# Two row groups of the last down weights on four DMA engines, in a two-layer decode kernel

## The chip, the cores and the metric

The kernel runs on one core of one Trainium2 chip. The metric is the device time of one execution in microseconds (us), the median of several runs. A core has TensorE (PE; its weight loads are PEld), VectorE (DVE), ScalarE (ACT), GpSimd (POOL) and SyncE (SP), and 16 DMA engines that bring data from HBM to SBUF. SyncE issues the loads here.

## The reference

Two sequences (B = 2) go through one token of two equal layers, each an attention over a cache (A) and a gated MLP (B), all in float32:

```python
x = x + _A_ref(_layernorm(x), A_k_cache, A_v_cache, A_wq, A_wo)   # 32 heads, 8192 keys, 128 wide
x = x + _B_ref(_layernorm(x), B_w_gate, B_w_up, B_w_down)         # 576 -> 4608 -> 576
x = x + _A_ref(_layernorm(x), A_k_cache, A_v_cache, A_wq, A_wo)
x = x + _B_ref(_layernorm(x), B_w_gate, B_w_up, B_w_down)

def _B_ref(x, w_gate, w_up, w_down):
    h = _gelu(x @ w_gate) * (x @ w_up)
    return h @ w_down
```

The same weights and caches serve both layers, and do not fit on the chip, so they are read twice: 1151 MB in all.

## The kernel before, in words

All loads go into one large buffer, `space` (128 partitions). A planner in Python, `Space`, holds a queue of loads with the place that each wants; `pump` issues the first of the queue as soon as the program that has been written so far frees its place, and never one ahead of another. So the order of the loads is the order in which they are put into the queue, and SyncE (which issues them) and the 16 DMA engines take them in that order. A load has one of eight semaphores in turn, so it also waits until the load eight issues before it has landed. The names in the rows of order below, DMAHW0 to DMAHW7, are these.

The change touches the very end, the down projection of the second layer. The hidden vector has 4608 numbers per sequence. They lie as 4 tiles (NT) of 128 partitions by 9 row groups (NI): hidden number t*1152 + 9*p + i is in tile t, partition p, group i. The weights of one row group of a tile are 128 rows of 576 (D) floats, one row a partition. `last_down` cuts the tiles into pieces, one load each: tile 0 whole (9 groups), tile 1 whole, tile 2 in two parts (groups 0 to 4, groups 5 to 8), tile 3 in five (0 to 3, 4 to 5, 6, 7, 8). `down` loads a piece: every partition of the 128 gets its groups one behind the other.

`lower` uses a piece up: for each group four matmuls, one for each 144 (CW) columns of the output, with the activations `hT` (128 partitions by 2 sequences) as weights and the piece as moving data, all added up in the PSUM bank `xps`. A float32 matmul counts as two instructions in the trace, each with a weight load. `hidden` makes `hT` from the sums of gate and up, on VectorE and ScalarE. `hT[1]` holds tiles 2 and 3. Line 996 adds `xps` to x, and two stores end the program.

`idle` lists fillers (line 990): matmuls on nothing of use, that keep TensorE busy behind a piece. Before, two of 256 columns stand behind the first part of tile 2, three behind the second, one of 160 behind the first part of tile 3.

Of the kernel before, what the change touches and what calls it, by code (L numbers as in the profile page):

```python
# [15 lines left out]
P = 128  # L16
B = 2
# [3 lines left out]
D = 576  # L21
# [4 lines left out]
HALF = P // 2  # L26
# [9 lines left out]
NI = 9  # L36
NT = 4
CW = D // 4
# [6 lines left out]

P0, P1, P2 = 0, 8 * PART, 16 * PART
HELD = 4 * DH
END = 25 * PART + 768 - HELD
MID = 19 * PART
MIDEND = END - 3 * PART + HELD  # L50
LATE = END - 4 * PART

# [79 lines left out]
def decode_layers(ctx, tc, x_in, kc, vc, wq, wo, wg, wu, wd, out):  # L132
    nc = tc.nc
# [6 lines left out]

    space = consts.tile([P, END], F32, name="space")
    sp = Space()
    at_of = {}
# [12 lines left out]
    def done(key):  # L156
        sp.free(key)
        sp.pump()
# [16 lines left out]
    def runs(where, a, n):  # L175
        return where.runs(a, n) if isinstance(where, Flow) else [(0, a, n)]

    def rows(key, w, width, where, first, size):

        def load(a):  # L180
            at_of[key] = a
            for off, to, n in runs(where, a, size):
                src = bass.AP(w.tensor, w.offset + first + off, [[18 * width, HALF], [10 * width, 2], [1, n]])
                nc.sync.dma_start(space[:, to:to + n], src)

        sp.queue.append((key, where, size, load))
# [34 lines left out]
    def down(key, where, piece):  # L221
        (t, lo), (last_t, _), n = piece[0], piece[-1], len(piece)

        def load(a):
            at_of[key] = a
            if last_t == t:
                src = wd[t * P * NI:(t + 1) * P * NI, :].rearrange("(p i) c -> p (i c)", i=NI)
                for off, to, m in runs(where, a, n * D):
                    nc.sync.dma_start(space[:, to:to + m], src[:, lo * D + off:lo * D + off + m])
            else:  # L230
                src = bass.AP(wd.tensor, wd.offset + (t * P * NI + lo) * D, [[NI * D, P], [P * NI * D, n], [1, D]])
                nc.sync.dma_start(space[:, a:a + n * D].rearrange("p (t c) -> p t c", t=n), src)

        sp.queue.append((key, where, n * D, load))

    def out_rows(key, where, g, lo=0, hi=GH):

        def load(a):
            at_of[key] = a
            src = wo[g * GH * DH:(g + 1) * GH * DH, :].rearrange("(p i) c -> p (i c)", i=GH)  # L240
            nc.sync.dma_start(space[:, a:a + (hi - lo) * D], src[:, lo * D:hi * D])

        sp.queue.append((key, where, (hi - lo) * D, load))
# [12 lines left out]
    def run(t, lo, hi):  # L256
        return [(t, i) for i in range(lo, hi)]

    first_down = [run(t, lo, lo + 3) for t in range(NT) for lo in range(0, NI, 3)]
    last_down = [run(t, 0, 9) for t in range(NT - 2)] + [run(NT - 2, *r) for r in ((0, 5), (5, 9))]  # L260
    last_down += [run(NT - 1, *r) for r in ((0, 4), (4, 6), (6, 7), (7, 8), (8, 9))]
    downs = first_down, last_down
    idle = {(1, NT - 2, 0): (256, 256), (1, NT - 2, 5): (256, 256, 256), (1, NT - 1, 0): (160,)}


    cache("k", 0, pairs[0], slots0[0], 0, 4)
# [26 lines left out]
    for g in range(NG):  # L293
        for lo in range(0, GH, 2):
            out_rows(("wo", 0, g, lo), mid, g, lo, lo + 2)
# [29 lines left out]
    for n, item in enumerate(pairs[::-1]):  # L325
        for m, kind in enumerate("kv"):
            at = slots1[(2 * n + m) % 3]
# [7 lines left out]
    for n, g in enumerate(range(NG)[::-1]):  # L335
        out_rows(("wo", 1, g, 0), n * GH * D if n < NG - 1 else P2, g)

    big = sp.ring(0, END)

# [4 lines left out]
    for off, n in ((0, 4), (4, 2), (6, 2)):  # L344
        rows(("u", 1, off), wu, HF, big, off * HF, n * HF)
    for piece in downs[1]:
        down(("d", 1) + piece[0], big, piece)


    ident = consts.tile([P, P], F32, name="ident")  # L350
# [60 lines left out]
    scores = consts.tile([P, P], F32, name="scores")  # L411
# [12 lines left out]
    sm = [psum1.tile([P, 512], F32, name="sm%d" % s) for s in range(2)]  # L424
    xps = psum1.tile([P, 512], F32, name="xps")
# [11 lines left out]
    def spin(bank, k=1):  # L437
        for _ in range(k):
            nc.tensor.matmul(bank[0:B, 3 * P:4 * P], of[:, 0:B], ident, start=True, stop=True)
# [52 lines left out]
    def attention(layer, items, apart):  # L492
# [134 lines left out]
        def base_of(kind, item, k):  # L627
            return at_of[key_of(kind, item, k)[:-1]] + k * PART

        def multiply(n, unit):  # L630
# [6 lines left out]
            at = base_of("k", item, lo)  # L637
            r0 = HELD // DH if layer == 1 and n == 0 and lo == 1 else 0
            to = at
# [166 lines left out]
        for n in range(last + 1):  # L806
# [4 lines left out]
            for k, unit in enumerate(units):  # L811
# [8 lines left out]
                if layer == 0 and n == last and k == 1:  # L820
                    sp.trim(("k", 0) + s3.name + (1,), HELD)
                if k == 0:
# [64 lines left out]
    def mlp(layer, apart):  # L887
# [13 lines left out]
        hT = [turns[:, 2 * NI * B * k:2 * NI * B * (k + 1)].rearrange("p (t r) -> p t r", r=B) for k in range(2)]  # L901
# [33 lines left out]
        def lower(piece):  # L935
            key = ("d", layer) + piece[0]
            for k, (t, i) in enumerate(piece):
                for c in range(4):
                    a = at_of[key] + k * D + c * CW
                    a = a if layer else flow.fold(a)  # L940
                    nc.tensor.matmul(
                        xps[32 * c:32 * c + B, 0:CW], hT[t // 2][:, t % 2 * NI + i, :], space[:, a:a + CW],
                        start=piece == downs[layer][0] and k == 0,
                        stop=piece == downs[layer][-1] and k == len(piece) - 1,
                    )
            done(key)

        if layer == 0:
            for half in range(2):
                for g, name in enumerate("gu"):  # L950
                    for i in range(NW):
                        for s in range(2):
                            key = name, 0, half, i, s
# [11 lines left out]
        else:  # L965
# [16 lines left out]
            for half in range(2):  # L982
                hidden(half)
        flat = prz.rearrange("p g e r -> p (g e r)")
        for piece in downs[layer]:
            lower(piece)
            if layer == 0:
                spin(qp[1], 2 if piece == downs[0][-1] else 1)
            for n in idle.get((layer,) + piece[0], ()):
                nc.tensor.matmul(sm[0][0:B, 0:n], hT[1][:, 0, :], flat[:, 0:n], start=True, stop=True)  # L990

    attention(0, forward, turn(True))
    mlp(0, turn())
    attention(1, backward, turn())
    mlp(1, turn())
    nc.vector.tensor_add(x, xps[:, 0:CW], x)
    for b, queue in enumerate((nc.sync, nc.scalar)):
# [28 lines left out]
```

## Time and profile before

| | us |
|---|---|
| median of three runs | 2684.74 |
| lowest and highest | 2684.34, 2685.34 |
| the profiled execution | 2684.92 |
| its span, from the first to the last instruction | 2683.1 |
| mean granted TensorE clock in it | 0.642 |

The profile is of one execution. Engine rows give the busy time, and in brackets what ended the idle time before. Rows of the windows view stand for one stretch of time each: its length, the busy time and count of PE, PEld, DVE, ACT and POOL, TensorE's granted clock as a share of full speed, the mean busy share of the 16 DMA engines, and what they moved in GB/s. The share is a mean: it tells how many engines work, not which. Rows with the name of a queue (q1 are the loads that SyncE issues) give packets, MB, and the share of the time of 16 engines.

### The profile page before, as it was taken

To read this page: it belongs to the slowest core of one execution; us is meant where nothing else is said; L and a number is where in the kernel's file an instruction comes from. 1 tells how busy PE (TensorE), PEld (TensorE's weight loads), DVE (VectorE), ACT (ScalarE), POOL (GpSimd) and SP (SyncE) were. 2 spreads that over 40 slices of the span, in tenths; PEclk is the share of its full clock that TensorE was granted. 3 is DMA by queue.
4 is the path that set the end of the run, shared out by engine and by line. 5 is a ranking of instruction groups with operands and counts; after the bars stand their busy time and mean duration, and the time that the engine had idled before them with its cause. 6 is when DMAs were issued, how large, how long until landed. Compare 5 with 4: busy or idle time off the path is not lost.

```text
span 2683.1 us, 18551 instructions
## 1 busy us (share of the span) xinstructions
PE 933.1 (35%) x7356; PEld 327.5 (12%) x7356; DVE 1864.7 (69%) x1358; ACT 180.8 (7%) x919; POOL 1143.3 (43%) x341
## 2 busy tenths in 40 slices
PE   1332332233233223326664233233323332332256
PEld 0110110011001101102221011001100110110022
DVE  5578777867777787787158777787677778767851
ACT  0000000000000000003013100000000000000000
POOL 2345444544544454454014444454454445435530
PEclk7656665666566566656986666566656656665667
DMA  9999999999999999999999999999999999999998
GB/s 422 435 436 427 433 435 433 434 430 434 432 433 434 431 432 437 433 427 421 406 407 442 430 429 434 436 434 425 436 437 432 430 434 434 432 434 430 433 424 374
DMA packets 37767, 1152.29 MB, mean 429 GB/s; under 512 B 4256, under 2 KB 4912, under 8 KB 16304
## 3 DMA queue, kind: packets, MB, share of 16 engines
q1 hardware_dynamic: 37656, 1151.09, 99.8%
q8 instruction: 58, 0.95, 0.1%
q14 instruction: 29, 0.24, 0.0%
q10 hardware_dynamic: 24, 0.01, 0.0%
HBM read 1151.08 MB, written 0.00 MB: 429 GB/s over the span
## 4 chain that ended last, share of the span: by engine, by line
DMA 26%; DVE 13%; PE 8%; POOL 6%; issue 1%; ACT 1%; POOLq 0%; SPq 0%; ACTq 0%; DVEq 0%
DMA space<-in_A_k_cache_dram 18%; DVE space L645 7%; POOL space L649 6%; PE acc L740 6%; DVE scores L662 4%; DMA space<-in_B_w_down_dram 3%; DMA space<-in_B_w_gate_dram 1%; DMA space<-in_B_w_up_dram 1%; DMA space<-in_A_v_cache_dram 1%; DMA space<-in_A_wo_dram 1%; DMA space<-in_A_wq_dram 1%; DVE osb L758 1%; ACT prz L710 1%; PE sm L720 0%; PE xps L785 0%
## 5 line engine op out<-in xcount | busy, mean ns | idle before, releaser
L649 POOL TENSOR_TENSOR space<-space 128x2048 f32<-128x2048 f32 (+3 forms) x331 | 1139.8, 3452 | 1314.2 <-DVE space L645 1183.8
L645 DVE TENSOR_TENSOR space<-space,qp 128x4096 f32<-128x4096 f32 (+1 forms) x331 | 1133.1, 3439 | 462.1 <-DMA space<-in_A_k_cache_dram 448.3
L662 DVE TENSOR_REDUCE scores<-space 128x32 f32<-128x2048 f32 (+3 forms) x331 | 581.6, 1757 | 115.1 <-POOL space L649 112.2
L740 PE MATMUL acc<-space,prz 128*8 128x512 f32 x4096 | 593.0, 741 | 8.0 <-issue 6.4
L769 PE MATMUL spare<-small,osb 128*64 128x2 f32 (+1 forms) x528 | 70.8, 256 | 1197.3 <-ACT osb L760 1180.1
L769 PEld LDWEIGHTS spare<-small,osb 128*64 128x64 f32 (+1 forms) x528 | 65.2, 208 | 1213.9 <-ACT osb L760 1195.1
L740 PEld LDWEIGHTS acc<-space,prz 128*8 128x8 f32 x4096 | 113.3, 103 | 422.4 <-issue 418.1
L694 PE MATMUL sm<-ident,small 128*1 128x128 f32 x66 | 24.3, 368 | 329.0 <-DVE small L692 329.0
L760 ACT COPY osb<-osb 128x128 f32<-128x128 f32 x60 | 17.9, 298 | 1730.4 <-DVE osb L758 1730.4
L758 DVE SCALAR_TENSOR_TENSOR osb<-acc,small,osb 128x128 f32<-128x128 f32 x204 | 71.6, 351 | 7.2
L476 POOL TENSOR_TENSOR small<-small 128x2 f32<-128x2 f32 x4 | 2.8, 699 | 165.2 <-DVE small L475 165.2
L720 PE MATMUL sm<-small 128*128 128x2 f32 x120 | 34.9, 361 | 81.0 <-ACT prz L710 81.0
L652 ACT ACTIVATE space<-space 128x128 f32<-128x128 f32 x188 | 55.6, 297 | 64.5 <-DVE space L645 51.9
L710 ACT ACTIVATE prz<-scores,small 64x128 f32<-64x128 f32 (+1 forms) x136 | 53.3, 392 | 3.2
L694 PEld LDWEIGHTS sm<-ident,small 128*1 128x1 f32 x66 | 5.2, 79 | 339.2 <-DVE small L692 309.1
L701 PE MATMUL sm<-small 1*128 1x2 f32 (+1 forms) x132 | 38.2, 356 | 22.7 <-DVE small L699 22.7
L720 PEld LDWEIGHTS sm<-small 128*128 128x128 f32 x120 | 29.8, 308 | 86.2 <-ACT prz L710 86.2
L699 DVE TENSOR_REDUCE small<-sm 1x2 f32<-1x128 f32 (+1 forms) x66 | 18.4, 279 | 31.1 <-PE sm L694 31.1
L756 DVE TENSOR_SCALAR osb<-acc,small 128x128 f32<-128x128 f32 x68 | 23.3, 342 | 23.7 <-PE acc L740 23.7
L706 ACT ACTIVATE small<-sm 128x2 f32<-128x2 f32 (+1 forms) x66 | 11.3, 172 | 390.1 <-PE sm L701 390.1
L701 PEld LDWEIGHTS sm<-small 1*128 1x128 f32 x132 | 32.5, 304 | 40.9 <-DVE small L699 40.7
L913 DVE STREAM_TRANSPOSE turned<-acc 128x288 f32<-128x288 f32 x4 | 1.9, 483 | 49.3 <-PE acc L895 49.2
(159 smaller groups left out, 448.1 us busy)
## 6 DMA issues: line engine op xcount, KB each, us to landing
space<-in_A_k_cache_dram SPq DMA_DIRECT2D x8, 4096.0 KB, 15.0
space<-in_A_v_cache_dram SPq DMA_DIRECT2D x3, 4096.0 KB, 20.9
space<-in_A_v_cache_dram SPq DMA_DIRECT2D x6, 2048.0 KB, 20.8
space<-in_B_w_gate_dram SPq DMA_DIRECT2D x18, 576.0 KB, 8.4
space<-in_B_w_up_dram SPq DMA_DIRECT2D x18, 576.0 KB, 7.8
space<-in_A_wo_dram SPq DMA_DIRECT2D x16, 576.0 KB, 8.1
space<-in_A_wo_dram SPq DMA_DIRECT2D x8, 1152.0 KB, 31.2
space<-in_B_w_gate_dram SPq DMA_DIRECT2D x2, 4608.0 KB
```

Of the source, the lines that this page charges most:

```text
L645: nc.vector.tensor_tensor(out=u, in0=t, in1=qp_of(n)[:, 0:DH].unsqueeze(1).to_broadcast([P, j - r0, DH]), op=ALU.mult)
L649: nc.gpsimd.tensor_tensor(out=half, in0=half, in1=u[:, :m - r0, DH // 2:], op=ALU.add)
L652: nc.scalar.activation(row, row, AF.Copy, accum_out=S[n][:, 16 * lo + r:16 * lo + r + 1])
L662: nc.vector.tensor_reduce(out=S[n][:, r0:r1], in_=half, axis=AX.X, op=ALU.add)
L694: nc.tensor.transpose(peaks[n], m, ident)
L701: nc.tensor.matmul(low[n], one[0:1, :].to_broadcast([1, P]), m1, start=True, stop=True)
L710: nc.scalar.activation(prz[rows_, 0:item.rows // 4, e, :], s[rows_, 0:item.rows].rearrange("p (g r) -> p g r", r=4), AF.Exp, bias=nbs[rows ...
L720: nc.tensor.matmul(tot, ones, rs[:, n % 2, :], start=True, stop=True)
L740: nc.tensor.matmul(acc_of(n)[32 * c:32 * c + 8, :], prz[:, g, :, :].rearrange("p e r -> p (e r)"), space[:, at:at + 4 * DH], start=(g < 4) ...
L756: nc.vector.tensor_scalar_mul(t, q[:, 0, :], diag[:, 0:1])
L758: nc.vector.scalar_tensor_tensor(t, q[:, r, :], diag[:, r:r + 1], t, op0=ALU.mult, op1=ALU.add)
L769: nc.tensor.matmul(to[:, i, 0:item.heads], t[:, i:item.heads * DH:GH], w, start=True, stop=True,)
```

## The change

Groups 7 and 8 of tile 2 (FEW = 2) leave the second piece of that tile. `few_rows` brings them to 32 partitions instead of 128: two loads, j = 0 and 1, each to 16 partitions (0 to 15 and 32 to 47), where each partition gets four pieces of 1152 floats, from four rows of the source that follow each other. The source is laid out as 4 x 16 x 1152, so that its outer dimension is 4. They stand in the queue between the two parts of tile 2.

The weights are now in other partitions, so the activations have to go there too. `choose_few` does it, ahead of tile 1: eight small matmuls with every fourth column of the unit matrix as weights pick out the activations of 16 partitions at a time into a PSUM bank, and two copies on VectorE bring them to `few`, a part of the `scores` buffer, which was cleared ahead. `lower_few`, ahead of the second part of tile 2, is then 32 matmuls of 48 partitions (16 to 31 count as zero) instead of 8 of 128. The fillers behind tile 2's parts go, and six of 256 columns stand behind tile 0.

```diff
+FEW = 2
...
+    def few_rows(key, where, t):
+
+        def load(a):
+            at_of[key] = a
+            for j in range(2):
+                first = (t * P + j * HALF) * NI + NI - FEW
+                src = bass.AP(wd.tensor, wd.offset + first * D, [[16 * NI * D, 4], [NI * D, 16], [1, FEW * D]])
+                nc.sync.dma_start(space[32 * j:32 * j + 16, a:a + 4 * FEW * D], src)
+
+        sp.queue.append((key, where, 4 * FEW * D, load))
...
-    last_down = [run(t, 0, 9) for t in range(NT - 2)] + [run(NT - 2, *r) for r in ((0, 5), (5, 9))]
+    last_down = [run(t, 0, 9) for t in range(NT - 2)] + [run(NT - 2, *r) for r in ((0, 5), (5, NI - FEW))]
...
-    idle = {(1, NT - 2, 0): (256, 256), (1, NT - 2, 5): (256, 256, 256), (1, NT - 1, 0): (160,)}
+    idle = {(1, 0, 0): 6 * (256,), (1, NT - 1, 0): (160,)}
...
     for piece in downs[1]:
+        if piece[0] == (NT - 2, 5):
+            few_rows(("few", 1), big, NT - 2)
         down(("d", 1) + piece[0], big, piece)
...
+        few = scores[:, 0:4 * FEW * B].rearrange("p (s i b) -> p s i b", i=FEW, b=B)
+
+        def choose_few():
+            nc.vector.memset(few, 0.0)
+            every = sm[1][:, 0:4 * FEW * B].rearrange("p (s i b) -> p s i b", i=FEW, b=B)
+            for j in range(2):
+                for s in range(4):
+                    nc.tensor.matmul(
+                        every[32 * j:32 * j + 16, s, :, :].rearrange("p i b -> p (i b)"),
+                        ident[:, HALF * j + s:HALF * j + HALF:4],
+                        hT[1][:, NI - FEW:NI, :].rearrange("p i b -> p (i b)"), start=True, stop=True,
+                    )
+                nc.vector.tensor_copy(few[32 * j:32 * j + 16], every[32 * j:32 * j + 16])
+
+        def lower_few():
+            at = at_of["few", 1]
+            for s in range(4):
+                for i in range(FEW):
+                    for c in range(4):
+                        a = at + (s * FEW + i) * D + c * CW
+                        nc.tensor.matmul(
+                            xps[32 * c:32 * c + B, 0:CW], few[0:48, s, i, :], space[0:48, a:a + CW],
+                            start=False, stop=False,
+                        )
+            done(("few", 1))
+
         for piece in downs[layer]:
+            if layer == 1 and piece[0] == (1, 0):
+                choose_few()
+            if layer == 1 and piece[0] == (NT - 2, 5):
+                lower_few()
             lower(piece)
```

How this moves the loads on SyncE, from the first part of tile 2 (128x2880) on; first the rows of before.

```order
L229 DMA space<-in_B_w_down_dram 128x2880 [waits DMAHW6_49,DVE_49,PE_49]
L229 DMA space<-in_B_w_down_dram 128x2304 [waits DMAHW7_49,DVE_49]
L229 DMA space<-in_B_w_down_dram 128x2304 [waits DMAHW0_49]
L229 DMA space<-in_B_w_down_dram 128x1152 [waits DMAHW1_49]
L229 DMA space<-in_B_w_down_dram 128x576 [waits DMAHW2_49,PE_49]
L229 DMA space<-in_B_w_down_dram 128x576 [waits DMAHW3_49,PE_49]
L229 DMA space<-in_B_w_down_dram 128x576 [waits DMAHW4_49,PE_49]
```

And the same place of the changed kernel, again on SyncE.

```order
L230 DMA space<-in_B_w_down_dram 128x2880 [waits DMAHW6_49,DVE_49,PE_49]
L244 DMA space<-in_B_w_down_dram 16x4x1152 [waits DMAHW7_49,DVE_49]
L244 DMA space<-in_B_w_down_dram 16x4x1152 [waits DMAHW0_49]
L230 DMA space<-in_B_w_down_dram 128x1152 [waits DMAHW1_49]
L230 DMA space<-in_B_w_down_dram 128x2304 [waits DMAHW2_49,PE_49]
L230 DMA space<-in_B_w_down_dram 128x1152 [waits DMAHW3_49,PE_49]
L230 DMA space<-in_B_w_down_dram 128x576 [waits DMAHW4_49,PE_49]
L230 DMA space<-in_B_w_down_dram 128x576 [waits DMAHW5_49,PE_49]
L230 DMA space<-in_B_w_down_dram 128x576 [waits DMAHW6_49,PE_49]
```

The two loads of 16 partitions stand ahead of what is left of tile 2, and each load behind them waits for a semaphore that is two places further on: the last two now for DMAHW5 (tile 1) and DMAHW6 (first part of tile 2).

On TensorE, behind tile 0, the rows of before: tile 1 from the wait for DMAHW5 on, tile 2, and its fillers (L990).

```order
L941 MATMUL xps<-space,turns 2x144 [waits DMAHW5_49]
L941 MATMUL xps<-space,turns 2x144 x35
L941 MATMUL xps<-space,turns 2x144 [waits DMAHW6_49,DVE_49]
L941 MATMUL xps<-space,turns 2x144 x15
L941 MATMUL xps<-space,turns 2x144 [waits Pool_49]
L941 MATMUL xps<-space,turns 2x144 x3
L990 MATMUL sm_112<-prz,turns 2x256 x2
L941 MATMUL xps<-space,turns 2x144 [waits DMAHW7_49]
L941 MATMUL xps<-space,turns 2x144 x10
L941 MATMUL xps<-space,turns 2x144 [waits Pool_49]
L941 MATMUL xps<-space,turns 2x144 x4
L990 MATMUL sm_112<-prz,turns 2x256 x3
```

The same place of the changed kernel, from the last rows of fillers behind tile 0 (L1034) to the end of tile 2; L1006 is `choose_few`, L1019 `lower_few`, `scores` holds `few`.

```order
L1034 MATMUL sm_112<-prz,turns 2x256 x5
L1006 MATMUL sm_113<-turns,ident 16x4 x4
L1006 MATMUL sm_113<-turns,ident 16x4 [waits DVE_49]
L1006 MATMUL sm_113<-turns,ident 16x4 x3
L955 MATMUL xps<-space,turns 2x144 [waits DMAHW5_49]
L955 MATMUL xps<-space,turns 2x144 x35
L955 MATMUL xps<-space,turns 2x144 [waits DMAHW6_49]
L955 MATMUL xps<-space,turns 2x144 x15
L1019 MATMUL xps<-space,scores 2x144 [waits DMAHW7_49,DMAHW0_49,DVE_49]
L1019 MATMUL xps<-space,scores 2x144 x10
L1019 MATMUL xps<-space,scores 2x144 x20
L955 MATMUL xps<-space,turns 2x144 [waits DMAHW1_49]
```

Between tile 0 and tile 1 there are now fillers and the eight matmuls of `choose_few`, with a wait for VectorE's first copy in their middle; behind the first part of tile 2 the moved groups take the place of two fillers.

## The prediction

> **What bounds the kernel now.** I read the page first, its DMA parts above all. (The first row names the span. Under 3 stand queue: packets, MB, share of the time of 16 DMA engines.)
>
> ```profile
> span 2683.1 us, 18551 instructions
> ...
> PE 933.1 (35%) x7356; PEld 327.5 (12%) x7356; DVE 1864.7 (69%) x1358; ACT 180.8 (7%) x919; POOL 1143.3 (43%) x341
> ...
> q1 hardware_dynamic: 37656, 1151.09, 99.8%
> q8 instruction: 58, 0.95, 0.1%
> ...
> HBM read 1151.08 MB, written 0.00 MB: 429 GB/s over the span
> ```
>
> The loads (q1) fill 99.8% of 16 engines' span, and no compute engine is over 69%. So the kernel is bound by DMA from end to end, and one DMA engine moves 429/16 = 26.8 GB/s. What is left to look at is the end. The chain that ended last:
>
> ```profile
> 2659.16 20.18 DMA space<-in_B_w_down_dram
> 2679.34 0.04 issue
> 2679.38 0.47 PE xps L941 x8
> 2679.85 0.02 issue
> 2679.87 0.31 DVE x L996
> ```
>
> The last row group of the down weights lands at 2679.34, eight TensorE instructions use it up, and one addition follows. Nothing but the arrival of the last bytes sets the end. Now the same end second by second; the last two columns are the mean share of 16 DMA engines that is busy, and GB/s, and the column before them is TensorE's granted clock.
>
> ```profile
> 2621.00:2671.00 50.00, 29.01 (x382) 12.00 (x374) 6.53 (x31) 0.47 (x2) 0.70 (x1) 0.70 1.00 423
> 2671.00:2672.00 1.00, 1.00 (x32) 0.64 (x26) 0.00 (x0) 0.00 (x0) 0.00 (x0) 0.70 0.98 394
> 2672.00:2673.00 1.00, 1.00 (x30) 0.60 (x19) 0.00 (x0) 0.00 (x0) 0.00 (x0) 1.00 0.82 336
> 2673.00:2674.00 1.00, 1.00 (x29) 0.71 (x31) 0.00 (x0) 0.00 (x0) 0.00 (x0) 1.00 0.66 270
> 2674.00:2675.00 1.00, 1.00 (x17) 0.54 (x13) 0.00 (x0) 0.00 (x0) 0.00 (x0) 1.00 0.59 228
> 2675.00:2676.00 1.00, 1.00 (x13) 0.31 (x14) 0.00 (x0) 0.00 (x0) 0.00 (x0) 1.00 0.58 217
> 2676.00:2677.00 1.00, 1.00 (x34) 0.77 (x26) 0.00 (x0) 0.00 (x0) 0.00 (x0) 1.00 0.55 217
> 2677.00:2678.00 1.00, 0.94 (x23) 0.36 (x24) 0.00 (x0) 0.00 (x0) 0.00 (x0) 1.00 0.18 71
> 2678.00:2679.00 1.00, 0.72 (x16) 0.17 (x16) 0.00 (x0) 0.00 (x0) 0.00 (x0) 1.00 0.11 41
> 2679.00:2680.00 1.00, 0.52 (x12) 0.11 (x8) 0.13 (x1) 0.00 (x0) 0.00 (x0) 1.00 0.06 16
> ```
>
> All 16 engines work until 2671 or so. Then the share falls in steps: 0.59 of 16 is nine engines, 0.11 is two. So **seven engines are done between 2671.5 and 2674.5, seven more near 2677, and two go on to about 2678.8**. All have the same bytes to move; they end 7 us apart. The shares after 2671 add up to 4.53 us: with the bytes dealt out evenly all would end at 2675.5, some 3.3 us before the last does now. **No shifting of bytes among engines can gain more than that**, 0.12% of the span.
>
> **The change, part by part.** The times are those of the profiled execution: 2683.1 us of span in a run of 2684.92, against a median of 2684.74 for three runs. I work out differences and set them off from the median.
>
> *The bytes.* One row group is 128 x 576 floats, 294,912 bytes, 18,432 for each of 16 engines. Every engine loses two: 36,864 bytes / 26.8 GB/s = **-1.38 us**. The same 589,824 bytes now go over four engines, 147,456 each: +5.50 us. So twelve engines end 1.38 us earlier, and **four end 4.12 us later**. The whole -1.38 is won if the four were done by 2678.8 - 1.4 - 4.1 = 2673.3; from there the gain shrinks, and one of the four that was done later than 2678.8 - 4.1 = 2674.7 makes the kernel slower.
>
> [...]
>
> *Which engines are early.* PE's 7,356 matmuls and as many weight loads are 14,712 instructions, and queue 8 carries 0.95 MB, which is 64 bytes for each: it fetches TensorE's program, 16 KB at a time. In the last 29 us the DMA view says of it:
>
> ```profile
> q8 instruction: 3, 0.05, 0.7%
> ```
>
> 0.7% of 16 x 29 us is 3.2 us for three packets, 1.1 us each, on the one engine that takes it. 58 of them are some 62 us of engine time, and an engine that is never idle does not catch up. Spread over all 16 they would delay all alike by 3.9 us; on eight of them, by 7.7 us each, which has the size of the 7 us between early and late. So I take it that eight engines bear the fetches and eight are nearly free of them. No view numbers the engines. [...]
>
> *Issue.* SyncE issues two loads more. It runs far ahead of the engines, except for the last pieces, which wait for the load eight issues before them. (The second and third row below are waits for the first part of tile 2, by SyncE, and for tile 1, by ScalarE, in front of the stores of the output.)
>
> ```profile
> 2625.57 33.92 SPq L229 DMA_DIRECT2D space<-in_B_w_down_dram  x9
> ...
> L998 SPq EVENT_SEMAPHORE  x1: 17/17/17, 2670.3 to 2670.3; - x1
> L998 ACTq EVENT_SEMAPHORE  x1: 17/17/17, 2666.8 to 2666.8; - x1
> ```
>
> With two loads more in the ring of eight, the last two row groups now wait for tile 1 (2666.8) and the first part of tile 2 (2670.3). The last engines need them at about 2676.7, the early ones could use them at 2669; an early engine may idle for 2 us and is still early. Cost: nothing, hidden by the 7 us of spread; without that cover 2 us. Both new loads go out before 2642 in any case, as the fourth and fifth of that row did.
>
> *TensorE and VectorE.* Rows that price the new instructions (each matmul counts as two):
>
> ```profile
> 2659.23 4.50 PE L941 MATMUL xps<-space,turns 128*2 128x144 f32 x72 [4.13 <-DVE mine L925]
> 2666.82 5.92 PE L941 MATMUL xps<-space,turns 128*2 128x144 f32 x112 [3.09 <-DMA space<-in_B_w_down_dram]
> 2674.42 1.46 PE L990 MATMUL sm<-prz,turns 128*2 128x256 f32 x6
> 2675.84 1.16 PE L941 MATMUL xps<-space,turns 128*2 128x144 f32 x32
> 2676.82 0.43 PE L990 MATMUL sm<-prz,turns 128*2 128x160 f32 x2
> ...
> 2608.63 1.12 PE L769 MATMUL spare<-small,osb 128*64 128x2 f32 x8
> ...
> 2612.94 0.17 DVE L462 COPY x<-x 128x16 f32<-128x16 f32 x1
> ...
> 2679.87 0.31 DVE L996 TENSOR_TENSOR x<-xps,x 128x144 f32<-128x144 f32 x1 [19.35 <-PE xps L941]
> ```
>
> A down instruction takes 4.50/72 = 0.063 us at half clock and 1.16/32 = 0.036 at full; a 256-wide filler 1.46/6 = 0.24 at full, 0.49 at half. Lowering the moved groups is 64 instructions instead of 16: 2.3 us instead of 0.6. Moving the activations is 16 small instructions, not shown before: between 0.036 and 0.14 us each (the row of L769, with four times the weight columns), 0.6 to 2.2 us; I take 1.4, nearer the first by size, and 0.4 for the copy between its two halves. VectorE's three small operations (0.17 each) lie in its 19.35 us of idle time.
>
> Now the order. Tile 0 ends at 2663.7. The fillers stand right behind it: in the run before, the clock rose some 4.8 us after work had begun at 2666.82 (0.70 in the second from 2671), so from 2659.2 it rises near 2664, if work goes on. Twelve filler instructions, 3.2 us: 2666.9. Activations: 2668.7. Tile 1, landed at 2666.8, 72 x 0.036 = 2.6: 2671.3. First part of tile 2, 1.4: 2672.7. Moved groups, 2.3: 2675.0 (they land by 2663.1 + 5.5 = 2668.6 on the earliest engine, and below 2672 on any early one). Then 0.6, 1.2, a filler of 0.4, 0.6: 2677.8, and three pieces of 0.3: 2678.7. Landing of the last group is 2679.34 - 1.38 = 2677.96. **So TensorE, which had slack, is a little late, and sets the end at 2678.7 instead of 2679.85**: of 1.38 us 1.15 are left. With the bounds of the small instructions it is 2677.9 to 2679.5, and not under 2677.96 + 0.47.
>
> Sum: -1.2 us, 2684.74 - 1.2 = **2683.5 us**.
>
> [...]
>
> **Rivals.**
> 1. *The four are mixed*: three early, one at 2674.5 or at 2677. It ends at 2678.6 or 2681.1, against 2678.8 now: -0.2 to +2.3 us, 2684.5 to 2687.0. For it: seven early ones, not eight, so one engine that the fetches spare is late for another reason and can be among the four.
> 2. *The loads spread over 16 engines after all*, since their target has 16 partitions. Then each engine moves what it moved, and nothing changes: 2684.7. Against it: the source of each load is laid out with four as its outer dimension, unlike every load of this trace.
> 3. *Slower: the four are among the nine late ones.* Place: the last packets on these queues. Price: 2678.8 + 4.1, 2688.8 us; it decides from an end after 2674.7 on. Over the bound of 0.2% (5.4 us) it goes only if the four also move 4.6 KB pieces at under four fifths of the rate. For it: nine of 16 are late. [...]
> 4. *TensorE becomes the bound*: the clock stays at half to 2671.6 as now. Fillers to 2669.3, activations to 2671, tile 1 to 2673.8, and on by the same rows to 2681.2: +1.3 us, 2686.1. Against it: twelve fillers close the 3.1 us gap in front of tile 1.
>
> **How the numbers follow.** Forecast 0.50; rival 1 0.22; rival 2 0.06; rival 3 0.12; rival 4 0.10. 0.2%, 5.4 us, is about what a measurement of this kernel can tell from no change. No case but a mishap of rival 3 goes over it upwards (0.03), and the 3.3 us of even dealing forbid it downwards (0.02 for what I do not see). The range goes from 2682.5 (all of 1.38 and 0.8 beside it) to 2687.0, the upper end of rival 1; most of rival 3 is left out.
>
> **What would show it.** Right: in the windows, the steps of the DMA share after 2671 move 1.4 us forward for the late engines and four of the early ones end near 2677; the last landing is at 2678.0 of the same clock; TensorE's gap in front of tile 1 is gone and the clock is 1.00 from 2666 on. The moved groups' wait on TensorE is short. Wrong: two to four engines alone busy after 2679 (rivals 1, 3); TensorE without a wait for DMA in its last three pieces and a clock of 0.50 to 2671 (rival 4); a share that falls as before (rival 2).

## The result, and the profile after

The changed kernel takes **2691.28 us** (median of 10 runs, 2690.54 to 2693.87) against 2685.10 us (10 runs of the kernel before on the same chip, 2684.34 to 2686.08): +6.2 us, ratio 1.0025, 95% interval 1.0015 to 1.0034. The forecast was 2683.5, the range ended at 2687.0, and "slower by over 0.2%" had 3 in 100. The profiled execution took 2692.85 us. From its page, the span, the row of the loads' queue and the bytes:

```profile
span 2691.1 us, 18691 instructions
...
q1 hardware_dynamic: 37816, 1151.09, 99.7%
...
HBM read 1151.08 MB, written 0.00 MB: 428 GB/s over the span
```

The bytes are the same, and the engines are about as full as before (99.7% against 99.8%). The packets tell how the new loads ran. There are 160 more than before. The two loads have 128 pieces; the other 32 are the packets that end a load, one on each engine that carries it: **sixteen for each load, not four**. (The page counts 32 packets more under 512 B, 4288 against 4256; by the trace's semaphore records each of the two loads updates its semaphore sixteen times, as an ordinary load does. The row reads so elsewhere: the kernel below with TensorE's work alone has one ordinary load more and 37,800 packets, 144 more, which are 128 pieces and 16 ends.) The premise "these bytes go over four engines" is false.

Now the end, in stretches. Columns as in the prediction's windows: length, busy PE, PEld, DVE, ACT, POOL, TensorE's clock, mean busy share of 16 DMA engines, GB/s.

```profile
2621.00:2662.00 41.00, 21.10 (x248) 7.26 (x252) 6.12 (x30) 0.47 (x2) 0.70 (x1) 0.75 1.00 426
2662.00:2671.00 9.00, 8.51 (x144) 5.16 (x140) 0.44 (x4) 0.00 (x0) 0.00 (x0) 0.80 1.04 266
2671.00:2676.00 5.00, 0.61 (x20) 0.25 (x12) 0.00 (x0) 0.00 (x0) 0.00 (x0) 0.98 0.93 145
2676.00:2679.00 3.00, 2.50 (x40) 1.31 (x40) 0.00 (x0) 0.00 (x0) 0.00 (x0) 0.50 1.00 370
2679.00:2683.00 4.00, 3.59 (x64) 2.19 (x64) 0.00 (x0) 0.00 (x0) 0.00 (x0) 0.50 0.68 273
2683.00:2687.00 4.00, 4.00 (x88) 2.30 (x80) 0.00 (x0) 0.00 (x0) 0.00 (x0) 0.61 0.13 46
```

Until 2662 nothing differs: share 1.00, 426 GB/s (425 in the kernel before). Then comes what no row shown of the kernel before has: **all engines busy and few bytes moved**, 266 GB/s for nine microseconds and 145 for five. The DMA view of those five:

```profile
DMA packets 169, 0.72 MB, mean 145 GB/s; under 512 B 27, under 2 KB 27, under 8 KB 153
...
q1 hardware_dynamic: 169, 0.72, 93.0%
```

Of 169 packets 153 are under 8 KB: the pieces of 4,608 bytes (those of the two loads, and of the ordinary 128x1152 load behind them) and the ends. The 169 hold the engines 93% of the time. From 2676 on the share falls in steps like those of the kernel before, some 7 us later.

The loss can be priced from these columns. An engine's rate is 429/16 GB/s, so busy time without its bytes is length x (share - GB/s / 429). Take 2662 to 2676 whole, of the kernel before and of the changed one:

```profile
2662.00:2676.00 14.00, 10.91 (x194) 6.15 (x186) 0.00 (x0) 0.00 (x0) 0.00 (x0) 0.66 0.89 368
```

```profile
2662.00:2676.00 14.00, 9.12 (x156) 5.41 (x148) 0.44 (x4) 0.00 (x0) 0.00 (x0) 0.87 1.00 222
```

Before: 14 x (0.89 - 0.858) = 0.5 us. After: 14 x (1.00 - 0.517) = 6.8 us. **The difference, 6.3 us, has the size of the +6.2 us between the medians.** But it is read from one execution, which took 7.9 us more than the profiled one of the kernel before (2692.85 against 2684.92). Of these, the rows from 2676 to 2683 hold another 0.6 us of the same kind; and TensorE ends 1.0 us behind the last landing (2686.82) instead of 0.5 behind it (2679.34). In the experiments below, length x (share - GB/s / 429) is called the empty busy time. It is always that of the profiled execution, and 0.5 us of it is in the kernel before too.

The two loads are not alone in being slow. The first part of tile 2 is an ordinary load to 128 partitions and stands ahead of them in the queue. It landed by 2670.3 in the kernel before; here it lands at 2676.46, and the chain that ended last runs through it (start, length):

```profile
2628.33 48.13 DMA space<-in_B_w_down_dram
```

The trace's packet records, which no view shows one by one, say the same: its 128 pieces of 11,520 bytes take 0.61 us each in the mean and up to 1.63, against 0.44 for every one of them in the kernel before.

TensorE in the same stretch (start, length, line, tiles, count, and in brackets the idle time ahead with what ended it):

```profile
2667.92 0.38 PE L1006 MATMUL sm<-turns,ident 128*16 128x4 f32 x8
2668.56 0.42 PE L1006 MATMUL sm<-turns,ident 128*16 128x4 f32 x8 [0.26 <-DVE scores L1011]
2669.22 2.39 PE L955 MATMUL xps<-space,turns 128*2 128x144 f32 x72 [0.24 <-DMA space<-in_B_w_down_dram]
2676.50 2.58 PE L955 MATMUL xps<-space,turns 128*2 128x144 f32 x40 [4.89 <-DMA space<-in_B_w_down_dram]
2679.50 4.02 PE L1019 MATMUL xps<-space,scores 48*2 48x144 f32 x64 [0.41 <-issue]
```

The moved activations cost 0.80 us. The first part of tile 2 comes so late that TensorE idles 4.89 us; its clock falls to 0.50 (windows from 2676), and what follows runs at half until 2686 or so. After that gap TensorE waits for a load only once more, 0.4 us in front of the moved groups (the second of the two loads lands at 2679.41). Is that a second loss, or only a follower of the first? The experiments had to say.

### The profile page after: what moved, and what is told of

Its sections match the earlier page's. It is cut to its first block, busy times and chain, and to the rows that moved or that the text cites. A ratio compares the mean times of both kernels' runs of the same rounds, so it can differ in the third digit from the quotient of the medians.

```text
span 2691.1 us, 18691 instructions
## 1 busy us (share of the span) xinstructions
PE 932.6 (35%) x7422; PEld 330.5 (12%) x7422; DVE 1864.9 (69%) x1361; ACT 180.9 (7%) x919; POOL 1143.4 (42%) x341
## 2 busy tenths in 40 slices
DMA packets 37927, 1152.29 MB, mean 428 GB/s; under 512 B 4288, under 2 KB 4944, under 8 KB 16592
## 3 DMA queue, kind: packets, MB, share of 16 engines
q1 hardware_dynamic: 37816, 1151.09, 99.7%
## 4 chain that ended last, share of the span: by engine, by line
DMA 26%; DVE 14%; PE 8%; POOL 6%; issue 1%; ACT 1%; POOLq 0%; SPq 0%; ACTq 0%; DVEq 0%
DMA space<-in_A_k_cache_dram 18%; DVE space L659 8%; POOL space L663 6%; PE acc L754 5%; DVE scores L676 4%; DMA space<-in_B_w_down_dram 3%; DMA space<-in_B_w_gate_dram 1%; DMA space<-in_B_w_up_dram 1%; DMA space<-in_A_v_cache_dram 1%; DVE osb L772 1%; DMA space<-in_A_wo_dram 1%; ACT prz L724 1%; DMA space<-in_A_wq_dram 1%; PE xps L955 0%; PE sm L715 0%
## 5 line engine op out<-in xcount | busy, mean ns | idle before, releaser
L754 PE MATMUL acc<-space,prz 128*8 128x512 f32 x4096 | 586.7, 735 | 8.1 <-issue 6.7
```

The source lines that it names most:

```text
L754: nc.tensor.matmul(acc_of(n)[32 * c:32 * c + 8, :], prz[:, g, :, :].rearrange("p e r -> p (e r)"), space[:, at:at + 4 * DH], start=(g < 4) ...
```

## The experiments

The theory, formed from the windows: sixteen engines that write into partitions 0 to 15 and 32 to 47 hold one another up, busy while they wait (a share of 0.93 at 145 GB/s), and what counts is which partitions they write to. Where they would wait, no view shows. The rivals: small pieces are slow anywhere; TensorE (64 instructions, half clock) makes the loss; the fillers do. Each time stands beside the median of the kernel before in the same comparison (2684.69, 2684.81 or 2684.75 us); an interval is that of the ratio.

**The fillers alone**, in the kernel before:

```diff
-    idle = {(1, NT - 2, 0): (256, 256), (1, NT - 2, 5): (256, 256, 256), (1, NT - 1, 0): (160,)}
+    idle = {(1, 0, 0): 6 * (256,), (1, NT - 1, 0): (160,)}
```

> The kernel before with the new list of fillers and nothing else: no load and no other instruction is changed. Theory (the two loads onto 32 partitions are slow because sixteen engines carry them into few partitions): the fillers cost nothing, 2685.1 us within 0.5, as TensorE waits for loads there. Rival 'shape' (small pieces are slow wherever they go): the same. Rival 'TensorE' (its 64 instructions and its clock make the loss): the same or up to 1 us less, since the clock rises earlier. Rival 'fillers' (the fillers themselves, or their instruction fetch, hold up the end): 2687 to 2691.

2685.63 us, +0.9 (0.9993 to 1.0011), at the edge of the range: no difference that can be told. Its TensorE shows where a part of a microsecond can go:

```profile
2666.57 2.44 PE L941 MATMUL xps<-space,turns 128*2 128x144 f32 x72
...
2672.82 1.16 PE L941 MATMUL xps<-space,turns 128*2 128x144 f32 x32 [1.38 <-DMA space<-in_B_w_down_dram]
2675.57 2.10 PE L941 MATMUL xps<-space,turns 128*2 128x144 f32 x32 [1.59 <-DMA space<-in_B_w_down_dram]
```

Tile 1 now runs at full clock (2.44 for 72). But with the fillers behind tile 2 gone the clock has fallen by 2675, and 32 instructions that took 1.16 us take 2.10. TensorE ends at 2680.6 instead of 2679.85.

**The TensorE work alone**: the two row groups come by one ordinary load onto 128 partitions; the activations are moved and the 64 instructions run as in the changed kernel.

```diff
-            for j in range(2):
...
-                nc.sync.dma_start(space[32 * j:32 * j + 16, a:a + 4 * FEW * D], src)
+            src = wd[t * P * NI:(t + 1) * P * NI, :].rearrange("(p i) c -> p (i c)", i=NI)
+            nc.sync.dma_start(space[:, a:a + FEW * D], src[:, (NI - FEW) * D:])
...
```

> The changed kernel with the two row groups loaded as every other row group, one load onto all 128 partitions, while TensorE still moves the activations and still does its 64 instructions on partitions 0 to 47 (on wrong rows, so the share of these two groups in the output is not the reference's). Theory (the loads are slow by their target): 2685 to 2686 us, the load's loss gone and at most 1 us of TensorE's work left at the end. Rival 'shape': the same. Rival 'TensorE': 2689 to 2691, its work being unchanged.

2684.89 us, +0.2 (0.9992 to 1.0010). The 64 instructions take 2.14 us at full clock, and TensorE again waits for the last row groups:

```profile
2671.70 2.14 PE L1017 MATMUL xps<-space,scores 48*2 48x144 f32 x64
...
2679.29 0.43 PE L953 MATMUL xps<-space,turns 128*2 128x144 f32 x8 [0.28 <-DMA space<-in_B_w_down_dram]
```

That is 0.1 under the expected range. So fillers, moved activations and 64 instructions together cost nothing that can be measured as long as the loads come in time. The loss is in the two loads.

**The same loads onto other partitions**, every fourth one, the first load in the lower half and the second in the upper:

```diff
-                nc.sync.dma_start(space[32 * j:32 * j + 16, a:a + 4 * FEW * D], src)
+                nc.sync.dma_start(space[HALF * j:HALF * j + HALF:4, a:a + 4 * FEW * D], src)
```

> The changed kernel with one edit: the same two loads, with the same sources, the same 128 pieces of 4,608 bytes and 16 target partitions each, but the targets are every fourth partition of the lower and of the upper half and no longer partitions 0 to 15 and 32 to 47. TensorE still reads partitions 0 to 47, so the share of these two row groups in the output is left out. Theory (few target partitions close together are what slows sixteen engines): most of the loss goes, 2685 to 2687 us, and GB/s no longer falls under 200 while all engines are busy. Rival 'shape' (pieces of 4,608 bytes, four for each engine and load, are slow anywhere): 2691 as the changed kernel. Rival 'TensorE' (64 instructions, clock at half): 2689 to 2691, because its work is the same.

2687.25 us, +2.6 (1.0000 to 1.0018), 0.25 over the range. Empty busy time 14 x (1.00 - 0.753) = 3.5 us, half of the changed kernel's:

```profile
2662.00:2676.00 14.00, 11.31 (x225) 6.93 (x218) 0.33 (x2) 0.00 (x0) 0.00 (x0) 0.87 1.00 323
```

Sources, pieces, number of target partitions and TensorE's instructions are the same, and more than half of the loss is gone: the rival "shape" falls.

**One load onto partitions 0 to 31, 0 to 63, or every fourth of all.** My estimate for the first two was a loss like the +2.6 us just measured, 2686 to 2688.5 us. The first:

```diff
...
+            src = bass.AP(wd.tensor, wd.offset + first * D, [[NI * D, P], [1, FEW * D]])
+            nc.sync.dma_start(space[0:32, a:a + 4 * FEW * D], src)
...
```

> The same two row groups, the same 128 pieces of 4,608 bytes, again into 32 partitions of four pieces each, but by one load into partitions 0 to 31 instead of two into 0 to 15 and 32 to 47; the activations are moved to fit, and TensorE still has its 64 instructions. [...] Rival 'closeness' (neighbouring partitions get in one another's way): 32 partitions in one row are as close as can be, 2691 as the changed kernel, or more. Rival 'number of target partitions' (32 in all, whichever): fallen already by the load on every fourth partition, and would give 2691 here.

The second has `space[0:64, a:a + 2 * FEW * D]`:

> The same two row groups by one load into partitions 0 to 63, two pieces each (32 TensorE instructions). [...] Rival 'number of target partitions': half the crowd of 0 to 31; its loss is halved, under 1.3 us, 2685 to 2686.

The third has `space[0:P:4, a:a + 4 * FEW * D]`:

> One load of the same 128 pieces of 4,608 bytes into 32 partitions of four pieces each, as in the run into partitions 0 to 31, but into every fourth partition from 0 to 124. TensorE still reads partitions 0 to 31, so the share of these two row groups in the output is left out. [...] Rival 'number of target partitions' (32 instead of 128): 2689, as in the run into 0 to 31. Rival 'pieces of four to a partition' : 2689 as well.

Measured: 2689.12 us (+4.3, 1.0007 to 1.0025), 2689.77 us (+5.0, 1.0009 to 1.0027) and 2685.36 us (+0.6, 0.9993 to 1.0011). The same stretch, first of 0 to 31, then of 0 to 63, then of every fourth:

```profile
2662.00:2676.00 14.00, 10.64 (x204) 6.99 (x200) 0.16 (x1) 0.00 (x0) 0.00 (x0) 0.87 0.99 303
```

```profile
2662.00:2676.00 14.00, 10.26 (x188) 5.89 (x180) 0.17 (x1) 0.00 (x0) 0.00 (x0) 0.87 0.99 311
```

```profile
2662.00:2676.00 14.00, 12.21 (x256) 8.10 (x252) 1.38 (x8) 0.23 (x1) 0.00 (x0) 0.88 0.98 402
```

Empty busy time: 4.0, 3.7 and 0.6 us. The first two are 0.6 and 1.3 us over the estimate. But 64 partitions are no better than 32, and 32 spread over all 128 cost about what an ordinary load does (+0.6 against +0.2). It is not the number of partitions that decides, but which ones they are. "Closeness" falls too: 0 to 31 is the closest set and costs less than 0 to 15 with 32 to 47.

The packet records give the same order without a rate. Summed over the last down loads and divided by 16 engines, the packets take longer than in the run with TensorE's work alone, which has as many pieces of each size, by 6.6 us in the changed kernel, 2.9 with every fourth partition of each half, 3.3 with 0 to 31, 3.2 with 0 to 63 and 0.0 with every fourth of all. (The profiled execution of the last took 2687.91 us, 2.6 over its median; what made it so long is not in these packets.)

What sets these partitions apart from one another was not shown: the runs give their order alone.

**Half the bytes**: `FEW = 1` in the changed kernel. My estimate was half its loss, 2687.5 to 2688.5 us.

> The changed kernel with one row group moved instead of two (pieces of 2,304 bytes, as many of them; 32 TensorE instructions instead of 64). [...] Rival 'a cost per load or per piece' (loads, pieces and their ends are as many as before): 2690 to 2692.

2688.63 us, +3.8 (1.0005 to 1.0023), 0.1 over the estimate. Loads, pieces and ends are as many (37,816 packets again), so a price per piece alone would have left the loss at 6.2; it falls with the bytes. The empty busy time is 14 x (1.00 - 0.734) = 3.7 us, 3.2 more than in the kernel before and half of the 6.3:

```profile
2662.00:2676.00 14.00, 11.14 (x224) 6.81 (x216) 0.31 (x2) 0.00 (x0) 0.00 (x0) 0.90 1.00 315
```

**The loads ahead of all last down weights**, so that TensorE never waits for them (my estimate was that the loss stays, 2689.5 to 2692 us):

```diff
-        if piece[0] == (NT - 2, 5):
+        if piece[0] == (0, 0):
             few_rows(("few", 1), big, NT - 2)
```

> The changed kernel with its two loads ahead of all last down weights instead of ahead of the last piece of tile 2, so that they land some 20 us earlier; TensorE uses them where it did. [...] Rival 'TensorE' (the wait for these loads in front of the end, the clock that falls in it, 64 instructions at half clock): 2685.5 to 2687. Rival 'it matters that the early engines are held up at the very end': 2686 to 2688, as the late engines would have the time to go on behind them.

2690.96 us, +6.2 (1.0014 to 1.0033). The empty stretch has moved forward with the loads, and its empty busy time is 16 x (1.02 - 0.613) = 6.5 us:

```profile
2648.00:2664.00 16.00, 6.80 (x76) 1.94 (x68) 3.62 (x16) 0.23 (x1) 0.00 (x0) 0.65 1.02 263
```

The 64 instructions run at full clock there (2.14 us), the last landing comes at 2686.52 as against 2686.82 in the changed kernel, and the time is the same. What the engines lose is not caught up: they have work until their last steps (a share of 0.99 from 2662 to 2676, 1.03 to 2679).

**More work for TensorE** in the changed kernel, by fillers behind tile 1:

```diff
-    idle = {(1, 0, 0): 6 * (256,), (1, NT - 1, 0): (160,)}
+    idle = {(1, 0, 0): 6 * (256,), (1, 1, 0): 10 * (256,), (1, NT - 1, 0): (160,)}
```

> The changed kernel with twenty more filler instructions behind tile 1, which close TensorE's gap of 4.9 us in front of tile 2 and hold its clock up. Loads unchanged. Theory: the loads' late end makes nearly all of the loss; the last landing stays where it was, and TensorE, now at full clock, ends 0.5 us behind it instead of 1.0: 2690.3 to 2691.3 us. Rival 'TensorE' (the cold clock, at half from 2676 to 2686, is a large part of the loss): 2686 to 2689.

2691.34 us, +6.6 (1.0016 to 1.0036), at the edge of the range and as the changed kernel. The gap was closed only in part (2.02 us are left, and the 64 instructions still take 4.02), but the first part of tile 2 now runs at full clock, and TensorE ends 0.5 us behind the last landing instead of 1.0. (Its last landing is at 2685.36 by the semaphore records, that of the changed kernel at 2686.82; one profiled execution each.) These 0.5 us don't show in the medians. This run alone leaves the clock of the 64 instructions as it was; with the run before, where they had full clock and the time stayed, the cold clock is a follower of the late loads.

**Loads that do run on four engines**: an outer step that the second dimension doesn't continue.

```diff
-                first = (t * P + j * HALF) * NI + NI - FEW
-                src = bass.AP(wd.tensor, wd.offset + first * D, [[16 * NI * D, 4], [NI * D, 16], [1, FEW * D]])
+                first = (t * P + j * 16) * NI + NI - FEW
+                src = bass.AP(wd.tensor, wd.offset + first * D, [[32 * NI * D, 4], [NI * D, 16], [1, FEW * D]])
...
```

> The changed kernel with loads that do run on four engines: the source's outer step is made 32 rows instead of 16, so that the two outer dimensions don't follow on one another and can't be taken as one of 64; the target partitions stay 0 to 15 and 32 to 47. The rows go to other partitions, and the moving of the activations is made to fit (eight more small copies on VectorE). Theory (sixteen engines into few partitions): four engines with four partitions each have no one beside them; each moves its 147 KB at its 26.8 GB/s, and the time is that of the prediction's own cases, 2683.5 us if the four are early ones, up to 2689 if they are late ones. Rival 'shape': the four move small pieces slowly, at under half the rate, and end 5 us or more after the others, 2689 and above. Rival 'TensorE': 2689 to 2691, its work being the same. What tells that four engines carry them: 24 packets fewer than in the changed kernel (8 instead of 32 for the ends of the loads).

2688.19 us, +3.5 (1.0005 to 1.0022). Its row of the loads:

```profile
q1 hardware_dynamic: 37792, 1151.09, 99.7%
```

136 packets more than before, 128 pieces and 4 ends for each load: four engines. In the trace's semaphore records each load gets one early update, 1.1 to 1.2 us after its issue, and four as it lands, where the loads of the changed kernel get sixteen; each of the four ends the second load 2.8 us behind the first, 73,728 bytes at 26 GB/s. Into the very partitions where sixteen engines crawl (145 GB/s in all), four go at nearly the mean rate of the whole span, 26.8 GB/s each. The empty busy time, 14 x (0.92 - 0.876) = 0.6 us, is that of the kernel before:

```profile
2662.00:2676.00 14.00, 11.10 (x228) 7.21 (x220) 1.39 (x13) 0.03 (x1) 0.00 (x0) 0.87 0.92 376
...
2677.00:2678.00 1.00, 1.00 (x24) 0.44 (x12) 0.00 (x0) 0.00 (x0) 0.00 (x0) 0.50 0.34 125
2678.00:2679.00 1.00, 1.00 (x23) 0.53 (x20) 0.00 (x0) 0.00 (x0) 0.00 (x0) 0.50 0.16 65
2679.00:2680.00 1.00, 1.00 (x24) 0.60 (x19) 0.00 (x0) 0.00 (x0) 0.00 (x0) 0.50 0.09 35
2680.00:2681.00 1.00, 1.00 (x28) 0.63 (x20) 0.00 (x0) 0.00 (x0) 0.00 (x0) 0.63 0.06 25
```

The loss here is of the other kind, that of rivals 1 and 3: one or two engines are left alone at the end (0.09 and 0.06 of sixteen), and the last row group lands at 2681.88, 2.5 us later than in the kernel before. TensorE, with its 64 instructions at half clock from 2674.24 on, ends another 0.7 us behind.

**Four engines, half the bytes**: the same with `FEW = 1`.

> The kernel with loads that run on four engines, with one row group moved instead of two: each of the four gets 73.7 KB more and 18.4 KB less, 2.06 us net, the other twelve end 0.69 us earlier; TensorE has 32 instructions instead of 64. By the ends that the four would have had (2673.1, 2674.7, 2675.7, 2677.7 worked out from the run with two row groups): the latest of the four lands at 2679.8, 0.4 us after the last of the kernel before, so 2685 to 2686 us. If four engines are slowed by anything but their bytes, 2687 and above.

2686.45 us, +1.7 (0.9996 to 1.0014): half the loss again, though the interval does not exclude no change, and 0.5 us over what was expected. The last landing is at 2680.9, not 2679.8; what made the 1.1 us between was not tried.

**Which engines are early?** Two tiny loads of 64 bytes to a partition stand behind the last load of the kernel before, the first into 4 partitions, the second into 8; nothing uses them. By their semaphore updates they ran on four engines and on eight.

```diff
...
+            nc.sync.dma_start(space[0:k, a:a + 16], bass.AP(wd.tensor, wd.offset, [[NI * D, k], [1, 16]]))
...
+    probe(("probe", 4), 4)
+    probe(("probe", 8), 8)
```

> [...] Forecast's theory: the four ends of the first tiny load come between 2671.5 and 2674.5 on the span's clock, with the seven early ones. Rival 'mixed' (the run on four engines: their ends less the 4.12 us of the added bytes would be 2673.1, 2674.7, 2675.7 and 2677.7): one to three of the four after 2675, among or near the late ones. Time in both cases 2685 us within 1.5.

2684.84 us, +0.1 (0.9992 to 1.0011). By the semaphore records the first tiny load ended on its four engines at 2672.75, 2674.79, 2675.38 and **2677.84**; the second on its eight at 2672.81, 2672.93, 2674.12, 2674.96, 2675.56, 2677.55, 2677.64 and 2678.03. The last row group of that run landed on seven engines between 2672.2 and 2675.2 and on nine between 2677.3 and 2679.2. So three of the four are early and one is late, and of the eight, five and three. The late one of the four fits the run on four engines, if these are the same four, which no view tells: 2677.84 + 4.12 = 2681.96, and its last landing was at 2681.88.

## Why the prediction was wrong, step by step

- *Bound by DMA to the end; seven engines early; at most 3.3 us to be won*: not contradicted. The probe sees the same seven and nine, and no variant came out ahead of the kernel before.
- **The bytes ("four engines end 4.12 us later") is the step that failed.** That a source with an outer dimension of four puts these loads on four engines was a premise, and no run shows its +5.50 us for them: 32 packets end the two, sixteen each. The sixteen engines were in the mean busy for 6.3 us more than their bytes need, and the last row group landed 7.5 us later than before, not 1.38 earlier. The source's dimensions [4, 16] with steps of 16 rows and one row are 64 rows on end, and in the run that has them on end they did not make four engines; with a step of 32 rows, 8 packets end the two loads, four each.
- *Rival 2 (sixteen engines after all, 0.06) had the right premise and the wrong price.* "Each engine moves what it moved, and nothing changes": 2684.7. The bytes per engine did stay; what changed was where they went. Measured: +6.2, with 6.3 us of empty busy time. The prediction worked out how many engines a load takes and never asked which partitions it fills.
- *The four are early*: the probe's load of four rows had three early and one late, 2677.84. Had the loads run on four engines, rival 1 would have been the case, with its upper end of +2.3 us; in the run that does use four, the last landing came out at +2.5, the median at +3.5.
- *Instruction fetch sorts the engines into early and late*: not tried. The probe has five early ones among its eight and two among the rest; the cause of that split stays open.
- *Issue costs nothing*: held as far as it can be seen. The last row group went out only when the first part of tile 2 had landed, at 2676.5, but the engines were busy until 2679.
- *TensorE*: the sizes held (activations 0.80 us for 1.4 taken and 0.6 to 2.2 bounded; 64 instructions 2.14 at full clock for 2.3; with the fillers alone the clock rose in the second from 2664, 0.85 in it and 0.50 in the one ahead, as worked out). That it would set the end came true in small, but for another reason: at half clock behind the late loads it ends 1.0 us behind the last landing instead of 0.5. The fillers' new place leaves the clock to fall at 2675 (0.50 in that second with the fillers alone), which the prediction didn't see.

**Where the loss lies, and what stays open.** The packet records answer the first in part. Of the 6.6 us by which the last packets take longer than in the run with TensorE's work alone, the pieces of 4,608 bytes, the two loads' own among them, make 3.6, and the longer pieces, all of ordinary loads, 3.0. So the loads in flight beside the two are held up as well. How one holds up the other was not tried, nor why 0 to 31 and 0 to 63 (+4.3 and +5.0) cost so much and every fourth of all (+0.6) next to nothing. The median with every fourth partition of each half is lower (+2.6), but it was taken on another chip, the intervals overlap, and the three profiled executions are alike (2688.25, 2688.04 and 2687.99 us), so that two loads are cheaper than one is not shown.

## What to carry to other kernels

Before giving a load fewer target partitions, ask two questions of it: on how many engines it runs, and which partitions these engines write to; the first alone says little: the same bytes on sixteen engines cost +6.2 us into 0 to 15 with 32 to 47 and +0.6 into every fourth of all. A DMA share of 1.00 is no proof that bytes move, as it stood beside 222 GB/s here: hold it against GB/s, and length x (share - GB/s / mean rate of the span) prices the loss in microseconds. And two outer dimensions that follow on one another may not run as the source code has them: count the packets that end a load to see how many engines took it (32 for two loads with a step of 16 rows, 8 with a step of 32).

## What the runs showed of the hardware

- Sixteen engines into 32 partitions, 0 to 15 and 32 to 47, moved 145 GB/s at a busy share of 0.93; four engines into the same partitions made 26 GB/s each. The stretch of 145 GB/s holds other loads too.
- Loads in flight beside them slow down too: pieces of 11,520 bytes of an ordinary load ahead of them took 0.61 us in the mean and up to 1.63, against 0.44.
- The same 589,824 bytes cost +6.2 us into 0 to 15 with 32 to 47, +4.3 into 0 to 31, +5.0 into 0 to 63, +2.6 into every fourth of each half by two loads, +0.6 into every fourth of all by one.
- Engines of one kernel end 7 us apart (2672.2 to 2679.2 in the probe), and the four that the probe's load of four rows ran on are spread over it: 2672.75 to 2677.84.
